# Fill pieces in cycles of four attention steps

## The chip, the cores and the metric

The kernel runs on one core of a Trainium2 chip. The metric is the time of one execution on the device, in microseconds (us). TensorE does the matmuls, ScalarE the exponentials, VectorE and GpSimd (POOL in the profile) the elementwise work; SyncE (SP) and GpSimd issue transfers.

## The reference

Two layers, each an attention block and a Fourier block, on x of 2048 rows and 640 columns, in fp32. There are 32 heads of 20 columns.

```python
def _A_ref(x, wqkv, wo):
    qkv = (x @ wqkv).reshape(B, S, 3, H, Dh).transpose(2, 0, 3, 1, 4)
    q, k, v = qkv[0], qkv[1], qkv[2]
    scores = jnp.einsum("bhqd,bhkd->bhqk", q, k) * (Dh ** -0.5)
    p = softmax(scores, axis=-1)
    o = jnp.einsum("bhqk,bhkd->bhqd", p, v)
    return o.transpose(0, 2, 1, 3).reshape(B, S, D) @ wo

def _B_ref(x, dft_seq_re, dft_seq_im, dft_hid_re, dft_hid_im):
    a = jnp.einsum("bsd,ed->bse", x, dft_hid_re)
    b = jnp.einsum("bsd,ed->bse", x, dft_hid_im)
    return jnp.einsum("ts,bse->bte", dft_seq_re, a) - jnp.einsum("ts,bse->bte", dft_seq_im, b)

for _ in range(2):
    x = x + _A_ref(layernorm(x), wqkv, wo)
    x = x + _B_ref(layernorm(x), dft_seq_re, dft_seq_im, dft_hid_re, dft_hid_im)
```

## The kernel before

A layer begins with a prologue (layer norm, transposes, the first two chunks of q and k, the first half of v), goes on with the attention sweep, and ends with the output projection and the Fourier block. The change touches the sweep alone.

**Steps.** The sweep has 512 steps. A step is a group `g` of four heads, a query block `qb` of 512 rows and a key chunk `kc` of 128 rows; `kc` runs fastest, then `qb`, then `g`. So a query block has 16 steps and a group has 64.

**Scores.** A step has two score tiles (`scores(n, j)`, two heads each). A tile is two matmuls at line 518, 62 rows deep and 512 columns wide, into one of three PSUM places `p0` to `p2`. ScalarE makes the exponential of the tile at line 521, into one of seven slots `e0` to `e6`. A score tile can start when the exponential of the third tile before it has left its place; an exponential can start when the values of the seventh tile before it have been taken.

**Values.** `values(n)` multiplies the exponentials of a step with v (line 529), for four heads side by side, and adds them up in `acc` over the 16 steps of a query block. In the program these are four matmuls for a step; the profile shows eight. At the last step `finish` transposes, divides and writes the block out.

**Fill work.** Only part of q, k and v exists when the sweep begins. The generator `work` makes the rest in pieces, on TensorE, between the steps: eight chunks of 128 columns of q or k, for four blocks of 512 rows each (15 matmuls of 512 columns for one block), and the second half of v, for 16 row tiles (15 matmuls of 320 columns for each). A piece is what `next(work)` issues; `s.blocks` counts them. All use one PSUM place, `fill`. After the last piece of a q or k block VectorE makes the two parts and the squares (`keep`), and some steps later `after` issues a norm matmul (line 212) and a reduction, from which the bound of the scores is made. At the end of a chunk it also splits the next weights and fetches those after them.

**Order.** All instructions stand in the order in which the program issues them; each engine waits with semaphores. `sweep` goes through the steps: two score tiles; then `fill(n)`, which may issue a piece; then values of earlier steps. Up to step `THIN = 236` the pieces go by `marks` (16 pieces up to step 44, 74 up to step 236), a block's pieces close together; while a block is unfinished (`more`) the values of a step are left for the next one, so that two steps of values come together. From step 236 on a piece comes at three places of each query block, and values follow by another rule.

**Loads.** `begin` and `sweep` also issue, at fixed `kc`, the loads of the next q and k tiles (`qload`, `kload`) on SyncE's queue, and `need` issues pieces at once where a group's chunk isn't made in time. `LATE` holds the groups whose last q chunk need only have its first 512 rows when the group starts. For these the bound is made again for each query block, and the q tiles of the next block are loaded at `kc` 10, not 4. Before, `LATE` is (4, 6).

`compare` issues VectorE's check of the Fourier matrices, spread over the steps. It was called with `fill` by `between`.

Of the kernel before, what the change touches and what calls it, by code (L numbers as in the profile page):

```python
# [23 lines left out]
GUARD = 30.0  # L24
NP = NT // 2
NQ = NT // 4
LATE = (256 // (4 * DH) + 1, 512 // (4 * DH))
FIRST = (0, 1, 4, 5)
HD = D // 2
TOL = 2.0 ** -32  # L30
# [5 lines left out]
def mha_fnet_kernel(ctx, tc, x_in, wqk, wv, wo, seq, hid, nat_seq, nat_hid, out):  # L36
# [65 lines left out]
    def pieces(blocks, n):  # L102

        todo = [f for b in blocks for f in b]
        for i in range(0, len(todo), n):
            for f in todo[i:i + n]:
                f()
            yield i + n < len(todo)
# [23 lines left out]
    class Qkv:  # L132
# [248 lines left out]
        def work(s):  # L381

            order = [ND + 1, 1, ND + 2, 2, ND + 3, 3, ND + 4, 4]
            w = {0: s.w1}

            def chunk(i):
                c = order[i]
                for tb in range(NB):
                    p = bank("fill", [128, 512], "pqk")
                    for more in pieces([s.product(p, w[i], tb, dc) for dc in range(ND)], 8 if (i, tb) < (5, 1) else 5):  # L390
                        if more:
                            yield True
                    sq = s.keep(p, c, tb, True, s.fill)

                    def after():
                        s.norms(bank("fill", [H, 512], "pn"), c, tb, sq)
                        s.made.add((c, tb))
                        if tb == NB - 1:
                            s.made.add(c)
                            if i + 1 < len(order):  # L400
                                w[i + 1] = s.weights(s.fill("w", [2, ND, 128], F32R, "wqk"), order[i + 1], True)
                            if i + 2 < len(order):
                                s.fetch(order[i + 2])
                    yield after

            for i in range(4):
                yield from chunk(i)
            for t in range(NT):
                p = bank("fill", [128, HD], "pv")
                for more in pieces([s.value(p, t, dc) for dc in range(ND)], 8):  # L410
                    if more:
                        yield True
                s.own(p, t, 1, True)
                yield None
            s.made.add("v")
            for i in range(4, 8):
                yield from chunk(i)

            s.silent = True
            r = s.bounds()  # L420
            ok = const.tile([128, 1], F32, name="ok", bufs=2)
            V.tensor_scalar(ok[:H], r[:H, 2:3], (GUARD / SCALE) ** 2, None, op0=OP.is_le)

            def after():
                p = bank("fill", [1, 1], "pok")
                PE.matmul(p, ok[:H], one[:H], start=True, stop=True)
                V.tensor_scalar(s.flag, p, float(H), None, op0=OP.is_equal)
            yield after
# [25 lines left out]
    class Attention:  # L454
# [95 lines left out]
                    G.dma_start(s.o[k, h * DH:(h + 1) * DH, qb * 512:(qb + 1) * 512],  # L550
                                hl[k][32 * j:32 * j + DH])

        def sweep(s, shift, begin, fill):
            done = calm = 0
            for n, (g, qb, kc) in enumerate(s.steps):
                begin(n, g, qb, kc)
                last = qb == NB - 1
                if kc == (7 if last else 10 if g in LATE else 4) and not (last and g == H // 4 - 1):
                    s.qload(*((g, qb + 1) if not last else (g + 1, 0)), shift)
                if last and g + 1 < H // 4:  # L560
                    for f, j in {1: [(0, 0)], 9: [(0, 1)], 11: [(1, 0)]}.get(kc, []):
                        s.kload(g + 1, f, j)
                if qb == 0 and kc == 0 and g:
                    s.kload(g, 1, 1)
                s.scores(n, 0)
                s.scores(n, 1)

                more, owed = fill(n) and n >= 2 and n + 1 < len(s.steps), n - 1 - done  # L570
                if n < s.THIN:
                    if more and kc != 1:
                        continue
                    count = owed
                else:
                    if more and owed < 3:
                        calm = n + 2
                        continue
                    count = min(owed, 1)
                    if owed > 1 and (done + 1) % NT and n >= calm:  # L580
                        calm = n + 2
                        count = 2
                for _ in range(count):
                    s.values(done)
                    done += 1
            for n in range(done, len(s.steps)):
                s.values(n)

        def run(s, done, project, check):

            work, tasks, later = s.a.work(), s.a.vweights(1, s.a.fill, pause=[lambda: None] * 2), list(check)
            s.work, s.blocks, s.after, s.rest, s.more, s.landed = True, 0, None, 0, False, 0

            marks = ((0, 0), (44, 16), (s.THIN, 74))

            def due(n):
                for (n0, k0), (n1, k1) in zip(marks, marks[1:]):
                    if n < n1:
                        return s.blocks < k0 + (k1 - k0) * (n - n0) / (n1 - n0)
                return s.blocks < 74 or s.blocks >= 107 or (n - 1) % NT in (2, 7, 12)  # L600

            def block(n):
                try:
                    f = next(work)
                    s.blocks += 1
                    s.more = f is True
                    s.after = (n + (2 if n < s.THIN else 4), f) if f and not s.more else None
                    s.rest = s.after[0] + 2 if s.after else n
                except StopIteration:
                    s.work = False  # L610
                    tasks.extend(done())

            def fill(n):
                if s.after:
                    if n >= s.after[0]:
                        f, s.after = s.after[1], None
                        f()
                elif s.work and n >= s.rest and (s.more and n < s.THIN or due(n + 1)):
                    block(n)
                    s.rest = max(s.rest, n + 2)  # L620
                    return s.work and not s.a.silent

            def compare(n):


                if n < 8:
                    return
                for _ in range(2):
                    if not later or n < s.landed or (len(check) - len(later)) * 490 >= n * len(check):
                        break  # L630
                    task = later.pop(0)
                    if isinstance(task, tuple):
                        s.landed = n + 5
                        task = task[1]
                    task()

            def need(n, *keys):
                while not all(k in s.a.made for k in keys):
                    if s.after:
                        fill(s.after[0])  # L640
                    else:
                        block(n)

            def begin(n, g, qb, kc):


                if qb == NB - 1 and g + 1 < H // 4:
                    when, to = 0, g + 1
                    c0, c1 = to * 80 // 128, ((to + 1) * 80 - 1) // 128
                    keys = [c0, (c1, 0) if to in LATE else c1, ND + c0, ND + c1] + (["v"] if to >= 4 else [])  # L650
                else:
                    when, to, keys = 5, g, [(((g + 1) * 80 - 1) // 128, qb + 1)]
                if to != g or g in LATE and qb < NB - 1:
                    if kc == when:
                        need(n, *keys)
                        s.shift = s.a.bound(to, s.room)
                    if kc - when in (0, 3, 5):
                        next(s.shift)

                if tasks and n % 2 == 0 and n >= 16 and n % 64 < 54:  # L660
                    tasks.pop(0)()
                for f in project.early.get(n, []):
                    f()

            def between(n):
                more = fill(n)
                compare(n)
                return more

            s.sweep("b", begin, between)  # L670
            assert not s.work and not later and not tasks, (len(later), len(tasks))

        def general(s, done, project):
# [35 lines left out]
                for j in range(2):  # L709
                    s.kload(0, f_, j)  # L710
            s.qload(0, 0, "m")
            s.sweep("m", lambda *_: None, lambda *_: None)
            for f in sum(project.early.values(), []):
                f()

# [813 lines left out]
```

## Time and profile before

| | |
|---|---|
| median of 3 runs | 2512.57 us (2512.54 to 2512.91) |
| the profiled execution | 2511.93 us, of which the span in the profile is 2510.1 |
| granted TensorE clock, mean | 0.999 |
| TensorE busy | 2479.9 us of the span |
| ScalarE busy | 2133.1 us |
| VectorE busy | 980.2 us |
| exponentials | 2048, 1934.4 us busy together |

Busy time of TensorE counts matmuls that are pipelined, so what a group of matmuls costs is better read from the distance between starts. In the profile's rows PE is TensorE, ACT ScalarE, DVE VectorE; a row of the timeline gives the start, the time to the end of the last, the engine, the line, what is written and read, the shape and the count; in brackets the idle time before it and what ended that. A row of the windows gives, for a stretch, the busy time of each engine (and the count of instructions), the granted TensorE clock, the share of the transfer engines and GB/s.

### The profile page before, as it was taken

The numbers are of one execution on the slowest core, as the hardware profiler recorded it, in microseconds if no ns is written. First come the engines' busy times: TensorE is split into PE (matmuls) and PEld (weight loads), VectorE is DVE, ScalarE is ACT, GpSimd is POOL, SyncE is SP. The second block draws the span as 40 slices with busy tenths as digits, with TensorE's granted clock in tenths as the row PEclk, the third lists the DMA queues.
The fourth block names the chain that finished last, engine by engine and source line by source line (L and its number), as shares of the span: only waits on it lengthen the run. The fifth ranks groups of instructions, "written<-read, shape, count | busy, mean of one in ns | idle before, by whom it ended". The sixth has DMA issues, their size and how long they took to land. (4 is left out here: it accounts for less than half of the span.)

```text
span 2510.1 us, 43669 instructions
## 1 busy us (share of the span) xinstructions
PE 2479.9 (99%) x16350; PEld 1147.5 (46%) x16350; DVE 980.2 (39%) x2144; ACT 2133.1 (85%) x2430; POOL 524.1 (21%) x1028
## 2 busy tenths in 40 slices
PE   8999999999999999999999999999999999999998
PEld 7644434433333332249885444444433333322596
DVE  6245422234243333416753444223233333332275
ACT  6688899989999999985457888999899999999752
POOL 2012111111212212113321121111121122221233
PEclk9999999999999999999999999999999999999999
DMA  5224221223222224327553332212131322233355
GB/s 188 95 88 126 81 90 44 83 72 94 86 90 86 94 86 123 118 89 245 190 182 100 114 111 91 80 57 65 59 100 51 92 62 71 58 108 96 115 211 195
DMA packets 127241, 262.58 MB, mean 105 GB/s; under 512 B 28952, under 2 KB 53304, under 8 KB 127020
## 3 DMA queue, kind: packets, MB, share of 16 engines
q1 hardware_dynamic: 88428, 159.83, 19.7%
q0 software_dynamic: 38592, 99.85, 12.6%
q8 instruction: 132, 2.16, 0.4%
q14 instruction: 89, 0.73, 0.1%
HBM read 175.29 MB, written 84.26 MB: 103 GB/s over the span
## 5 line engine op out<-in xcount | busy, mean ns | idle before, releaser
L521 ACT ACTIVATE e<-psc 128x1024 f32<-128x1024 f32 x2048 | 1934.4, 1121 | 126.0 <-PE psc L518 94.1
L529 PE MATMUL acc<-e,v 128*32 128x512 f32 x8192 | 1057.9, 602 | 3.9 <-DVE of L536 3.8
L518 PE MATMUL psc<-stq,stk 62*128 62x512 f32 x4096 | 786.2, 455 | 1.3 <-ACT e L521 1.3
L518 PEld LDWEIGHTS psc<-stq,stk 62*128 62x128 f32 x4096 | 335.5, 184 | 792.3 <-ACT e L521 762.6
L529 PEld LDWEIGHTS acc<-e,v 128*32 128x32 f32 x8192 | 188.9, 108 | 381.6 <-issue 358.4
L99 PE MATMUL pqk<-xt,wqk 128*128 128x512 f32 x1200 | 319.6, 407 | 2.1 <-DVE top L213 1.4
L550 POOL DMA_DIRECT2D o<-oh x256 | 131.5, 522 | 872.5 <-DVE oh L545 871.4
L84 DVE CAST hl<-pqk 128x512 fp32r<-128x512 f32 x64 | 44.3, 692 | 553.5 <-PE pqk L99 553.5
L99 PEld LDWEIGHTS pqk<-xt,wqk 128*128 128x128 f32 x1200 | 213.2, 188 | 90.3 <-issue 43.5
L536 DVE STREAM_TRANSPOSE of<-acc 128x512 f32<-128x512 f32 x64 | 45.8, 716 | 349.9 <-PE acc L529 349.3
L99 PE MATMUL pv<-wv,xt 128*128 128x320 f32 x960 | 159.7, 316 | 0.0
L99 PEld LDWEIGHTS pv<-wv,xt 128*128 128x128 f32 x960 | 141.1, 188 | 24.7 <-issue 21.2
L550 POOL DMA_DIRECT2D o<-ot x256 | 128.5, 510 | 1.9 <-issue 1.4
L207 POOL DMA_DIRECT2D scrq<-hl x40 | 28.1, 704 | 446.1 <-DVE hl L87 311.4
L243 DVE COPY v<-pv 128x320 f32<-128x320 f32 x32 | 15.7, 491 | 235.3 <-PE pv L99 235.3
L765 DVE TENSOR_REDUCE far<-cq 128x1 f32<-128x512 f32 (+5 forms) x169 | 98.5, 584 | 5.7
L92 PE MATMUL py<-wo,o 128*128 128x320 f32 x320 | 99.1, 310 | 1.4 <-DVE xr L947 1.4
L207 POOL DMA_DIRECT2D scrk<-hl x40 | 28.0, 699 | 344.3 <-DVE hl L87 300.2
L93 PE MATMUL py<-wo,o 128*128 128x320 f32 x320 | 98.6, 308 | 0.0
L94 PE MATMUL py<-wo,o 128*128 128x320 f32 x320 | 98.6, 308 | 0.0
L769 DVE TENSOR_TENSOR cq<-cq 128x512 f32<-128x512 f32 (+4 forms) x166 | 96.4, 580 | 2.4 <-DMA cq<-in_nat_seq_dram 2.4
L213 DVE TENSOR_REDUCE top<-pn 32x1 f32<-32x512 f32 x80 | 53.5, 676 | 107.4 <-PE pn L212 107.4
(200 smaller groups left out, 1729.2 us busy)
## 6 DMA issues: line engine op xcount, KB each, us to landing
cq<-in_nat_seq_dram POOLq DMA_DIRECT2D x64, 512.0 KB, 5.3
scrq<-hl POOLq DMA_DIRECT2D x40, 512.0 KB, 3.2
scrk<-hl POOLq DMA_DIRECT2D x40, 512.0 KB, 3.2
stq<-scrq SPq DMA_DIRECT2D x256, 80.0 KB
stk<-scrk SPq DMA_DIRECT2D x128, 160.0 KB
o<-o SPq DMA_DIRECT2D x16, 1280.0 KB
stq<-scrq SPq DMA_DIRECT2D x256, 40.0 KB
stk<-scrk SPq DMA_DIRECT2D x128, 80.0 KB
```

The costliest lines, as they stand in the source:

```text
L92: PE.matmul(out_ap, ah, bh, start=start, stop=False)
L93: PE.matmul(out_ap, ah, bl, start=False, stop=False)
L94: PE.matmul(out_ap, al, bh, start=False, stop=stop)
L99: yield lambda i=i, j=j, k=k: PE.matmul(out_ap, a[i], b[j], start=dc == 0 and k == 0, stop=dc == ND - 1 and k == 2)
L207: G.dma_start(s.scr["qk"[k]][c * 128:(c + 1) * 128, :, tb * 512:(tb + 1) * 512], hl.bitcast(F32))
L213: V.tensor_reduce(s.top[:H, c // ND, c % ND, tb:tb + 1], p, op=OP.max, axis=AX.X)
L518: PE.matmul(p[:, i], s.k[g, kc // 8, j][r, kc % 8 * 128:(kc % 8 + 1) * 128], s.q[g, qb, j][r], start=True, stop=True)
L521: A.activation(e, p, AF.Exp, scale=SCALE)
L529: PE.matmul(s.acc[32 * j:32 * j + 32], s.a.v[kc][:, v0:v0 + 32], s.e[n, j // 2][:, j % 2], start=kc == 0, stop=kc == NT - 1, skip_group_ch ...
L550: G.dma_start(s.o[k, h * DH:(h + 1) * DH, qb * 512:(qb + 1) * 512], hl[k][32 * j:32 * j + DH])
L765: V.tensor_reduce(to, x, op=OP.max, axis=AX.X, apply_absolute_value=True)
L769: V.tensor_tensor(y, x, y, op=op)
```

## The change

`sweep` takes a `plan`. Where `plan(n)` gives a piece, four steps go as one cycle: three score tiles, the piece, three score tiles, values of two steps, two score tiles, the waiting `after` if there is one, values of two steps. `plan` gives one at steps 1, 5, 9 and so on, up to step 229, for the first 58 pieces. A v block is one piece of 15 matmuls, not one of 8 and one of 7, so there are 58 pieces up to that point where there were 74. Pieces outside the cycles come from step 236 on, as before. `LATE` has group 1 too, since the chunk of its last head is made later than before.

```diff
-LATE = (256 // (4 * DH) + 1, 512 // (4 * DH))
+LATE = (1, 4, 6)
...
-                for more in pieces([s.value(p, t, dc) for dc in range(ND)], 8):
+                for more in pieces([s.value(p, t, dc) for dc in range(ND)], 15):
...
+            while n < len(s.steps):
+                opened(n)
+                piece = plan and plan(n)
+                if piece:
+
+                    for t in range(8):
+                        m, j = n + t // 2, t % 2
+                        if t and not j:
+                            opened(m)
+                        s.scores(m, j)
+                        if t == 2:
+                            piece()
+                        if t == 7:
+                            fill(m)
+                        if j:
+                            compare(m)
+                        if t in (5, 7):
+                            for _ in range(2):
+                                s.values(done)
+                                done += 1
+                    n += 4
+                    continue
                 s.scores(n, 0)
                 s.scores(n, 1)
                 more, owed = fill(n) and n >= 2 and n + 1 < len(s.steps), n - 1 - done
-                if n < s.THIN:
-                    if more and kc != 1:
-                        continue
-                    count = owed
+                compare(n)
+                n += 1
+                if plan and n <= s.THIN:
+                    count = owed + 1
+                elif more and owed < 3:
+                    calm = n + 1
+                    continue
...
-            marks = ((0, 0), (44, 16), (s.THIN, 74))
...
-                return s.blocks < 74 or s.blocks >= 107 or (n - 1) % NT in (2, 7, 12)
+                return s.blocks < 58 or s.blocks >= 91 or (n - 1) % NT in (2, 7, 12)
...
-                elif s.work and n >= s.rest and (s.more and n < s.THIN or due(n + 1)):
+                elif s.work and n >= max(s.rest, s.THIN) and due(n + 1):
...
+            def plan(n):
+                if n % 4 == 1 and n + 3 < s.THIN and s.blocks < 58 and not s.after:
+                    return lambda: block(n + 1)
...
-            s.sweep("b", begin, between)
+            s.sweep("b", begin, fill, plan, compare)
```

`opened(n)` holds what stood at the head of the loop: `begin` and the loads of a step.

More of the change, by code (lines that the diff above doesn't have):

```diff
@@ L551, in finish, with sweep, opened @@
                                 hl[k][32 * j:32 * j + DH])
-        def sweep(s, shift, begin, fill):
-            done = calm = 0
-            for n, (g, qb, kc) in enumerate(s.steps):
+        def sweep(s, shift, begin, fill=lambda n: None, plan=None, compare=lambda n: None):
+            done = calm = n = 0
+            def opened(n):
+                g, qb, kc = s.steps[n]
                 begin(n, g, qb, kc)
@@ L570, in sweep @@
                 more, owed = fill(n) and n >= 2 and n + 1 < len(s.steps), n - 1 - done
-                if n < s.THIN:
-                    if more and kc != 1:
-                        continue
-                    count = owed
-                else:
-                    if more and owed < 3:
-                        calm = n + 2
-                        continue
+                compare(n)
[5 more added lines that the diff above has]
+                    continue
+                else:
                     count = min(owed, 1)
-                    if owed > 1 and (done + 1) % NT and n >= calm:
-                        calm = n + 2
+                    if owed > 1 and (done + 1) % NT and n > calm:
+                        calm = n + 1
                         count = 2
@@ L592, in run @@
             s.work, s.blocks, s.after, s.rest, s.more, s.landed = True, 0, None, 0, False, 0
-            marks = ((0, 0), (44, 16), (s.THIN, 74))
             def due(n):
-                for (n0, k0), (n1, k1) in zip(marks, marks[1:]):
-                    if n < n1:
-                        return s.blocks < k0 + (k1 - k0) * (n - n0) / (n1 - n0)
-                return s.blocks < 74 or s.blocks >= 107 or (n - 1) % NT in (2, 7, 12)
+                return s.blocks < 58 or s.blocks >= 91 or (n - 1) % NT in (2, 7, 12)
             def block(n):
@@ L663, in begin @@
                     f()
[L665 to L668, printed above, removed]
-            s.sweep("b", begin, between)
+            s.sweep("b", begin, fill, plan, compare)
             assert not s.work and not later and not tasks, (len(later), len(tasks))
@@ L711, in general @@
             s.qload(0, 0, "m")
-            s.sweep("m", lambda *_: None, lambda *_: None)
+            s.sweep("m", lambda *_: None)
             for f in sum(project.early.values(), []):
```

## The prediction

> **What bounds the kernel now.** I read the page first, for the engine that is never idle.
>
> ```profile
> span 2510.1 us, 43669 instructions
> ...
> PE 2479.9 (99%) x16350; PEld 1147.5 (46%) x16350; DVE 980.2 (39%) x2144; ACT 2133.1 (85%) x2430; POOL 524.1 (21%) x1028
> ```
>
> TensorE at 99% may still be an average over stages with different limits, so the second view was the windows. I cut them at the first score matmul of step 0, at that of step 233 (the first step after the new cycles) and at the end of the sweep; the last row is the early window of the second layer.
>
> ```profile
> core 0: us, PE busy (x) PEld busy (x) DVE busy (x) ACT busy (x) POOL busy (x), PEclk, DMA share, GB/s
> 86.62:593.31 506.69, 503.61 (x3357) 208.83 (x3357) 184.86 (x375) 448.60 (x467) 87.69 (x156) 1.00 0.27 85
> 593.31:1117.20 523.89, 523.67 (x3543) 173.68 (x3539) 182.59 (x399) 518.87 (x559) 101.21 (x182) 1.00 0.30 93
> 1330.24:1837.20 506.96, 503.32 (x3357) 208.68 (x3357) 180.66 (x350) 448.87 (x467) 88.81 (x158) 1.00 0.28 86
> ```
>
> In the early window ScalarE works 448.60 of 506.69 us, TensorE nearly always. In the later one ScalarE works 518.87 of 523.89 us: there the exponentials are the limit. The changed cycles lie wholly in the early window, where TensorE's order decides; what follows keeps its limit. So a microsecond of TensorE time saved before step 233 moves all that follows by a microsecond, as long as ScalarE does not become the limit of the early window too.
>
> The third view is the timeline of TensorE alone, over two q/k pieces. Its columns are the start, the time to the end, and the count; what a group costs is the distance to the next start, since matmuls overlap.
>
> ```profile
> 99.89 2.11 PE L99 MATMUL pqk<-xt,wqk 128*128 128x512 f32 x8
> 101.92 0.73 PE L518 MATMUL psc<-stq,stk 62*128 62x512 f32 x4
> 102.59 1.92 PE L529 MATMUL acc<-e,v 128*32 128x512 f32 x16
> 104.44 0.73 PE L518 MATMUL psc<-stq,stk 62*128 62x512 f32 x4
> 105.10 1.88 PE L99 MATMUL pqk<-xt,wqk 128*128 128x512 f32 x7
> 106.91 0.73 PE L518 MATMUL psc<-stq,stk 62*128 62x512 f32 x4
> 107.57 1.92 PE L529 MATMUL acc<-e,v 128*32 128x512 f32 x16
> 109.43 0.73 PE L518 MATMUL psc<-stq,stk 62*128 62x512 f32 x4
> 110.09 0.39 PE L212 MATMUL pn<-sq,ind 128*32 128x512 bf16 x1
> 110.10 1.24 PE L529 MATMUL acc<-e,v 128*32 128x512 f32 x8
> 111.27 0.73 PE L518 MATMUL psc<-stq,stk 62*128 62x512 f32 x4
> 111.93 1.06 PE L529 MATMUL acc<-e,v 128*32 128x512 f32 x8
> 112.92 0.73 PE L518 MATMUL psc<-stq,stk 62*128 62x512 f32 x4
> ```
>
> From start to start: two score tiles 0.66 us (104.44 to 105.10); values of one step 0.99 (111.93 to 112.92), of two steps 1.85 (102.59 to 104.44); a q or k piece of eight 2.03 (99.89 to 101.92), of seven 1.81 (105.10 to 106.91); the norm matmul lengthens the values behind it from 0.99 to 1.17 (110.10 to 111.27), so 0.18. Two values together cost 0.13 less than twice one: a change from one kind of work to another costs something that a longer run does not pay again. That is what the change collects. The groups lie end to end; TensorE hardly waits here.
>
> **The new cycle, term by term.** A cycle is 3 score tiles, piece, 3 score tiles, 2 values, 2 score tiles, 2 values: four steps and one piece. By the order of TensorE's instructions there are 58 of them, steps 1 to 232: 21 with eight q/k matmuls, 21 with seven and a norm, 16 with a whole v block of fifteen. The same work was in 74 pieces before; the steps, tiles and matmuls are as many.
>
> A run of three score tiles stands in the trace near a layer's start, with a wait behind it that is needed below.
>
> ```profile
> 86.62 0.73 PE L518 MATMUL psc<-stq,stk 62*128 62x512 f32 x4
> ...
> 89.35 0.98 PE L518 MATMUL psc<-stq,stk 62*128 62x512 f32 x6
> 90.97 0.50 PE L518 MATMUL psc<-stq,stk 62*128 62x512 f32 x2 [0.65 <-ACT e L521]
> 91.40 1.88 PE L99 MATMUL pqk<-xt,wqk 128*128 128x512 f32 x7
> ...
> 93.87 1.92 PE L529 MATMUL acc<-e,v 128*32 128x512 f32 x16
> 95.73 0.73 PE L518 MATMUL psc<-stq,stk 62*128 62x512 f32 x4
> ```
>
> ScalarE in the same stretch:
>
> ```profile
> 87.19 1.94 ACT L521 ACTIVATE e<-psc 128x1024 f32<-128x1024 f32 x2
> 89.90 4.88 ACT L521 ACTIVATE e<-psc 128x1024 f32<-128x1024 f32 x5 [0.77 <-PE psc L518]
> 95.03 1.02 ACT L521 ACTIVATE e<-psc 128x1024 f32<-128x1024 f32 x1 [0.26 <-PE acc L529]
> 96.33 5.61 ACT L521 ACTIVATE e<-psc 128x1024 f32<-128x1024 f32 x6 [0.27 <-PE psc L518]
> ```
>
> Six score matmuls last 0.98, four 0.73: the third tile adds 0.25, so three tiles cost 0.66 + 0.25 = 0.91. The other bound for it is 0.33, half of a pair.
>
> A v block of fifteen is not in this sweep, but its halves are:
>
> ```profile
> 311.71 1.29 PE L99 MATMUL pv<-wv,xt 128*128 128x320 f32 x7
> 312.93 0.73 PE L518 MATMUL psc<-stq,stk 62*128 62x512 f32 x4
> ...
> 321.23 1.43 PE L99 MATMUL pv<-wv,xt 128*128 128x320 f32 x8
> 322.60 0.73 PE L518 MATMUL psc<-stq,stk 62*128 62x512 f32 x4
> ```
>
> Seven cost 1.22, eight 1.37; the eighth adds 0.15 by the starts and 0.14 by the lengths. Fifteen cost 1.22 + 8 x 0.145 = 2.38, against 2.59 for the halves.
>
> TensorE alone then needs 0.91 + P + 0.91 + 1.85 + 0.66 + 1.85 = 6.18 + P: 8.21 with eight, 7.99 with seven, 8.56 with a v block.
>
> ScalarE has to fit in. There are three score banks, so a cycle's sixth tile waits until the third tile's exponential has ended. The first exponential starts 0.60 after its score (95.73 to 96.33). Six in a row take 5.61, one alone 1.02, so each further one (5.61 - 1.02) / 5 = 0.918; the third ends at 0.60 + 2 x 0.918 + 1.02 = 3.46 after the cycle's start. At 90.97 a tile waited in this way for the exponential that began at 89.90 and ended at 90.92: it started 0.05 later. So the sixth tile may start at 3.51. TensorE would reach it at 0.91 + P + 0.58, where 0.58 is 0.91 less one tile: 3.52 with eight, no wait; 3.30 with seven, a wait of 0.21; 3.87 with a v block, none. From a tile that waited to what follows it is 0.43 (90.97 to 91.40), not 0.33. So the seven-cycle costs 3.51 + 0.43 + 4.36 = 8.30 (4.36 are the two pairs of values and the two tiles between them), not 7.99. This wait is new; behind it on TensorE stand those values and tiles, and nobody else waits for them but ScalarE.
>
> The sixth tile's exponential also needs one of the seven slots for exponentials, which the first values free 1.16 after they begin (93.87 to 95.03): at 3.94 + 1.16 = 5.10. ScalarE reaches it at 0.60 + 5 x 0.918 = 5.19 anyway. The eighth starts at 3.94 + 1.85 + 0.60 + 0.918 = 7.31, and ScalarE is free at 8.23, while the next cycle's first exponential is not ready before 8.30 + 0.60. These 0.7 us of slack in each cycle are why ScalarE does not set its length.
>
> The sum for a layer: 21 x (8.21 + 8.30 + 0.18) = 350.5 and 16 x 8.56 = 137.0, together 487.5. Step 0 runs ahead of the first cycle: five score tiles in a row, of which the fifth waits for the second exponential. That ends at 87.19 + 1.94 = 89.13, and 0.05 + 0.43 later the piece starts, at 89.61; in a settled cycle it starts 0.91 after the cycle, so step 0 costs 89.61 - 0.91 - 86.62 = 2.08. Step 233 then comes 489.6 us after step 0, where it took 506.69 and 506.96. **Gain: 17.1 and 17.4 us in the two layers, 34.5 in all.**
>
> **What else moves.** Behind step 233 there is no piece until step 237, as before, and the same work is left. The new order has one step of values fewer owed there, 0.85 us for each layer (1.85 - 0.99) if TensorE is still late at that point: not counted, kept for the lower end.
>
> The norm matmul waits for squares that VectorE makes of the piece. It comes 0.91 + 1.85 + 0.66 = 3.42 behind the seven, before 0.66 + 1.85 + 0.66 = 3.17. VectorE is busy 185 of 507 us in this window; if in that share of cases the norm came late by as much as it lasts, 0.39, it would be 21 x 0.36 x 0.39 = 2.9 us for each layer, an upper end. I take nothing, since the norms get more time than they had.
>
> A query block ends on the last values of a cycle, with six score tiles and the piece between them and the accumulator's next use, so its evacuation is hidden; with values of two blocks back to back it would stand between them. v is complete at step 192 and needed at step 240.
>
> Group 1's q tiles are late now: its bound is made again for each query block, three times more in a layer, and the loads are issued at step 10 of 16 and not 4, behind the bound's own transfer on SyncE's queue. Group 4 does that already:
>
> ```profile
> 655.30 0.24 SPq L499 DMA_DIRECT2D stq<-shiftb  x1
> ...
> 666.72 0.73 PE L518 MATMUL psc<-stq,stk 62*128 62x512 f32 x4
> ```
>
> The last of the twelve loads is issued at 655.30, the scores that need them start at 666.72: 11.4 us to spare, landing included. Group 1's blocks are no shorter (four cycles, 33 us). So I take nothing for it.
>
> The profiled execution took 2511.93 us for its span of 2510.1; the median of the runs is 2512.57. 2511.93 - 34.5 = 2477.4; on the median, 2512.57 - 34.5 = 2478.1. I forecast **2478 us**. Under 0.2% (5 us) could not be told from no change here.
>
> **Rivals.**
>
> *The ring of three banks does not bind* (12%): with the first exponential at 0.55 (89.35 to 89.90) instead of 0.60, or a restart that overlaps the wait, the seven-cycles come near 7.99. Worth up to 21 x 0.31 = 6.5 for each layer: 2465, and 2463 with the value step already done.
>
> *Longer runs save less* (17%): the third tile at 0.33 makes both runs of three 0.08 longer, 0.16 a cycle where no wait hides it, (21 + 16) x 0.16 = 5.9 for each layer: 2490. If the eight-cycles too pay the restart of 0.1, 2494; with late norms besides, 2500. For it: the three-tile run stands only once in a layer. Against it: its length of 0.98.
>
> *It is refilled* (3%): a further wait of 0.30 in each of the 58 cycles takes the whole gain, 2512. Exponentials that do not overlap, 1.02 each, would give all q/k cycles 0.60 + 2 x 1.02 + 1.02 + 0.05 + 0.43 + 4.36 = 8.50 and still leave 7 us of gain in each layer; nothing in the rows shows more.
>
> *Late q tiles* (5%), slower: three block starts of group 1 in each layer. Its loads share SyncE's queue with the weights' fetches, which wait for VectorE. They have 11 us to spare; beyond that each microsecond costs six, so 17 us later the gain is gone, and 22 us later the time is 2478 + 6 x 10.6 = 2542. Group 4's rows speak against it.
>
> *The clock falls* (3%), slower: were the wait in the seven-cycles to lower TensorE's clock to half, each microsecond at that clock would lose half of one. At 34 us of a layer's 490 the gain is gone; at a fifth of them, 98 us, the time is 2478 + 98 = 2576. Against it: the granted clock is 1.00 in all windows, the later one too, where TensorE's scores wait for ScalarE. The Trainium skill, "TensorE: Matmul & The Clock Gate", section "A second HAM failure mode: psum-queue depth-cycling", tells of small idle gaps between matmul groups, from cycling through the PSUM banks, that made the clock swing to half. By that rule the new order, with its wait on a bank, would be the slower one; the later window's 1.00 does not agree with it.
>
> **How the numbers follow.** Forecast 60%, its rivals 12, 17, 3, 5 and 3. Faster: 60 + 12 + 17 = 89%; same 3%; slower 8%. The range goes from 2463 (no bank wait, one value step less) to 2497 (the third tile at its bound, restarts, part of the late norms). It leaves out the last three rivals and the far ends of the first two, under two in ten.
>
> **What would show it.** Between the first scores of steps 0 and 233, 490 us instead of 507, in both layers; groups of six score matmuls 0.91 from start to start, a v block 2.38; a wait for the exponential ahead of the sixth tile in the seven-cycles, 0.2 us, and none in the v cycles; the stretch from step 233 on within 1 us of 523.9. A sixth tile that waits in all cycles, group 1's scores waiting for a transfer at a block's start, or a granted clock under 1.00 would make it wrong.

## The result, and the profile after

The changed kernel takes 2483.94 us (median of 4 runs, 2483.46 to 2485.32), the kernel before 2512.56 beside it: a ratio of 0.9887, 95% interval 0.987 to 0.9904. It is faster by 28.6 us, where 34.5 were forecast. The profiled execution has a span of 2481.4 us.

The windows of the changed kernel, cut at the same points as before: the first score matmul of step 0, that of step 233, and the end of the sweep, in both layers.

```profile
core 0: us, PE busy (x) PEld busy (x) DVE busy (x) ACT busy (x) POOL busy (x), PEclk, DMA share, GB/s
86.55:579.88 493.33, 490.26 (x3365) 220.08 (x3364) 188.09 (x391) 441.74 (x467) 90.91 (x161) 1.00 0.29 89
579.88:1103.53 523.65, 523.43 (x3531) 173.60 (x3530) 181.54 (x397) 518.48 (x558) 99.37 (x179) 1.00 0.30 92
1316.29:1808.16 491.87, 489.46 (x3365) 220.11 (x3365) 183.87 (x368) 442.20 (x467) 90.83 (x161) 1.00 0.29 90
1808.16:2331.90 523.74, 523.51 (x3533) 173.61 (x3532) 158.05 (x390) 518.48 (x558) 102.71 (x191) 1.00 0.25 74
```

The early windows are 13.4 and 15.1 us shorter (506.69 and 506.96 before), 28.4 together; the span is shorter by 28.7. The later windows have hardly moved (523.89 before, 523.65 and 523.74 now), and the clock stays at 1.00. So all but 0.3 us of the gain lies between step 0 and step 233, as forecast, and the question is only how long a cycle is there.

Two cycles on TensorE, one with eight matmuls and one with seven and a norm:

```profile
105.38 0.96 PE L518 MATMUL psc<-stq,stk 62*128 62x512 f32 x6
106.28 2.11 PE L99 MATMUL pqk<-xt,wqk 128*128 128x512 f32 x8
108.32 1.07 PE L518 MATMUL psc<-stq,stk 62*128 62x512 f32 x6
109.32 1.92 PE L529 MATMUL acc<-e,v 128*32 128x512 f32 x16
111.17 0.73 PE L518 MATMUL psc<-stq,stk 62*128 62x512 f32 x4
111.84 1.92 PE L529 MATMUL acc<-e,v 128*32 128x512 f32 x16
113.69 0.96 PE L518 MATMUL psc<-stq,stk 62*128 62x512 f32 x6
114.58 1.89 PE L99 MATMUL pqk<-xt,wqk 128*128 128x512 f32 x7
116.40 1.30 PE L518 MATMUL psc<-stq,stk 62*128 62x512 f32 x6
117.63 1.92 PE L529 MATMUL acc<-e,v 128*32 128x512 f32 x16
119.49 0.73 PE L518 MATMUL psc<-stq,stk 62*128 62x512 f32 x4
120.15 0.39 PE L212 MATMUL pn<-sq,ind 128*32 128x512 bf16 x1
120.16 2.10 PE L529 MATMUL acc<-e,v 128*32 128x512 f32 x16
122.19 0.97 PE L518 MATMUL psc<-stq,stk 62*128 62x512 f32 x6
```

A run of three tiles ahead of a piece lasts 0.96 to 0.97 and costs 0.89 to 0.90. The run behind the seven lasts 1.30: the wait that was forecast stands inside it (start to start 1.23, so 0.33 more than 0.90). The run behind the eight lasts 1.07 and costs 1.00, 0.10 more, where none was forecast. The eight-cycle is 113.69 - 105.38 = 8.31 us, the seven-cycle with its norm 122.19 - 113.69 = 8.50.

A v cycle has no such wait (its first three groups cost 0.89, 2.40 and 0.89), 367.12 - 358.57 = 8.55:

```profile
358.57 0.96 PE L518 MATMUL psc<-stq,stk 62*128 62x512 f32 x6
359.46 2.46 PE L99 MATMUL pv<-wv,xt 128*128 128x320 f32 x15
361.86 0.96 PE L518 MATMUL psc<-stq,stk 62*128 62x512 f32 x6
...
367.12 0.96 PE L518 MATMUL psc<-stq,stk 62*128 62x512 f32 x6
```

ScalarE over the same two q/k cycles: it goes through the piece with hardly a gap (eight exponentials in one row) and idles 0.6 to 0.7 us at a cycle's start.

```profile
105.98 7.73 ACT L521 ACTIVATE e<-psc 128x1024 f32<-128x1024 f32 x8 [0.74 <-PE psc L518]
114.29 5.61 ACT L521 ACTIVATE e<-psc 128x1024 f32<-128x1024 f32 x6 [0.58 <-PE psc L518]
120.12 1.94 ACT L521 ACTIVATE e<-psc 128x1024 f32<-128x1024 f32 x2 [0.22 <-PE psc L518]
122.78 2.86 ACT L521 ACTIVATE e<-psc 128x1024 f32<-128x1024 f32 x3 [0.73 <-PE psc L518]
```

### The profile page after: what moved, and what is told of

Same layout as the page of the kernel before. It is cut to its first block, busy times and chain, and to the rows that moved or that the text cites. A ratio compares the mean times of both kernels' runs of the same rounds, so it can differ in the third digit from the quotient of the medians.

```text
span 2481.4 us, 43743 instructions
## 1 busy us (share of the span) xinstructions
PE 2451.9 (99%) x16350; PEld 1170.1 (47%) x16350; DVE 984.7 (40%) x2174; ACT 2118.3 (85%) x2430; POOL 527.4 (21%) x1034
## 5 line engine op out<-in xcount | busy, mean ns | idle before, releaser
L529 PE MATMUL acc<-e,v 128*32 128x512 f32 x8192 | 1041.6, 601 | 0.4 <-DVE of L536 0.4
L518 PE MATMUL psc<-stq,stk 62*128 62x512 f32 x4096 | 770.4, 452 | 5.5 <-ACT e L521 1.9
L529 PEld LDWEIGHTS acc<-e,v 128*32 128x32 f32 x8192 | 207.7, 108 | 380.3 <-issue 348.6
L99 PE MATMUL pv<-wv,xt 128*128 128x320 f32 x960 | 151.3, 313 | 0.0
```

Of the source, the lines that this page charges most:

```text
L99: yield lambda i=i, j=j, k=k: PE.matmul(out_ap, a[i], b[j], start=dc == 0 and k == 0, stop=dc == ND - 1 and k == 2)
L518: PE.matmul(p[:, i], s.k[g, kc // 8, j][r, kc % 8 * 128:(kc % 8 + 1) * 128], s.q[g, qb, j][r], start=True, stop=True)
L529: PE.matmul(s.acc[32 * j:32 * j + 32], s.a.v[kc][:, v0:v0 + 32], s.e[n, j // 2][:, j % 2], start=kc == 0, stop=kc == NT - 1, skip_group_ch ...
```

## The experiments

In what follows a run is an unbroken row of matmuls of one kind on TensorE (scores, values, a piece, a norm). The theory: starting a run costs 0.1 to 0.2 us, the change starts fewer of them, and what it does not gain is taken by the sixth score tile's wait for the third exponential. Each kernel was timed beside the kernel before on the same chip, but not all on one chip: the kernel before took 2511.8 us beside four of them and 2512.6 to 2512.7 beside the others, so two rows compare to about 1 us. The stage is the time from the first score matmul of step 0 to that of step 233 in the profiles; the last column counts its runs in the order of TensorE's instructions.

| kernel | median us | ratio to before, interval | stage, layer 1 and 2 | runs in a stage |
|---|---|---|---|---|
| before | 2512.56 | | 506.7, 507.0 | 486 |
| changed | 2483.94 | 0.9887 (0.987 to 0.9904) | 493.3, 491.9 | 369 |
| v blocks whole, alone | 2519.57 | 1.0031 (1.0019 to 1.0042) | 508.9, 509.0 | 485 |
| group 1 late, alone | 2511.97 | 1.000 (0.999 to 1.0009) | 506.6, 506.9 | 486 |
| two tiles ahead of the piece | 2525.82 | 1.0055 (1.0038 to 1.0071) | 513.3, 513.8 | 485 |
| pieces of ten and five | 2496.46 | 0.994 (0.9923 to 0.9956) | 499.0, 499.0 | 369 |
| extra behind the 2nd exponential | 2492.53 | 0.9924 (0.9907 to 0.994) | 496.0, 496.2 | 369 |
| extra behind the 8th exponential | 2484.62 | 0.9887 (0.9871 to 0.9904) | 493.6, 492.1 | 369 |
| three tiles ahead, runs as many as with two | 2502.7 | 0.9961 (0.9946 to 0.9975) | 502.1, 502.1 | 485 |

**Pieces of ten and five** (against the changed kernel)

```diff
-... 8 if (i, tb) < (5, 1) else 5):
+... 10 if (i, tb) < (5, 1) else 5):
```

> The changed kernel with the fifteen matmuls of a q or k block cut into ten and five, not eight and seven; nothing else. The theory (a cycle is not shorter than 8.31, since its sixth score tile waits for the third one's exponential, which ends at 3.46): with ten the piece takes 2.51 and the cycle 0.89 + 2.51 + 0.89 + 4.36 = 8.65, with five TensorE needs 7.5 and waits up to 8.31. So 0.34 x 21 = 7.1 us more for each layer, 2498 in all, and a wait of 0.7 us ahead of the sixth tile in the five-cycles. A rival (TensorE's own work sets the length of all cycles, and what is missing of the forecast gain was lost elsewhere): the same matmuls in the same cycles, 2484.

```profile
105.91 0.96 PE L518 MATMUL psc<-stq,stk 62*128 62x512 f32 x6
106.81 2.56 PE L99 MATMUL pqk<-xt,wqk 128*128 128x512 f32 x10
...
114.56 0.96 PE L518 MATMUL psc<-stq,stk 62*128 62x512 f32 x6
115.45 1.42 PE L99 MATMUL pqk<-xt,wqk 128*128 128x512 f32 x5
116.81 0.85 PE L518 MATMUL psc<-stq,stk 62*128 62x512 f32 x4
118.07 0.50 PE L518 MATMUL psc<-stq,stk 62*128 62x512 f32 x2 [0.41 <-ACT e L521]
118.50 1.92 PE L529 MATMUL acc<-e,v 128*32 128x512 f32 x16
```

The ten-cycle takes 114.56 - 105.91 = 8.65 us. In the five-cycle the sixth tile stands apart, with ScalarE named for its wait; it starts 118.07 - 114.56 = 3.51 after the cycle's start, as it does behind seven and behind eight. The wait is 0.7 us, as expected: after the fifth tile the sixth could follow at 117.39, and comes at 118.07. The same matmuls in the same cycles cost 12.5 us more in all (14 expected). In the second layer's stage it is 7.2 us, where 7.1 was worked out; in the first it is 5.7, because five exponentials that start late in the changed kernel (below) start late here too, but ahead of ten matmuls, where they cost nothing. So a q/k cycle has a floor, and work under it is free.

**A small exponential more, in two places** (against the changed kernel)

```diff
                         s.scores(m, j)
+                        if t == 1:
+                            A.activation(extra, ident[:, :16], AF.Exp, scale=SCALE)
...
+    extra = const.tile([128, 16], F32, name="extra")
```

In the other kernel it is `t == 7`.

> The changed kernel with a small exponential more on ScalarE in each of the 58 cycles, behind the second tile's: 128 x 16 elements of a constant, which nobody reads. It takes x, 0.1 to 0.2 us. The theory (the third exponential's end holds the sixth score tile): each q/k cycle is longer by x, 8.31 + x, the v cycles, whose sixth tile comes 0.35 after that end, keep 8.56. 42 x x for each layer, with x = 0.15 that is 6.3, 12.6 in all: 2497 (2492 to 2501). A rival (TensorE is the limit and ScalarE has 0.7 us to spare in each cycle): 2484.

> The changed kernel with the same small exponential more in each cycle, but behind the eighth tile's, where ScalarE waits 0.5 us for the next cycle's first score. The theory: no change, 2484 within 1 us; where on ScalarE the time is added decides, not how much. A rival (ScalarE as a whole is close to the limit of the cycles): as behind the second, 2492 or more.

Behind the second, ScalarE and then TensorE:

```profile
107.00 1.94 ACT L521 ACTIVATE e<-psc 128x1024 f32<-128x1024 f32 x2 [0.74 <-PE psc L518]
108.83 0.22 ACT L579 ACTIVATE extra<-ident 128x16 f32<-128x16 f32 x1
108.93 5.89 ACT L521 ACTIVATE e<-psc 128x1024 f32<-128x1024 f32 x6
```

```profile
106.40 0.96 PE L518 MATMUL psc<-stq,stk 62*128 62x512 f32 x6
107.29 2.11 PE L99 MATMUL pqk<-xt,wqk 128*128 128x512 f32 x8
109.33 1.18 PE L518 MATMUL psc<-stq,stk 62*128 62x512 f32 x6
...
114.81 0.96 PE L518 MATMUL psc<-stq,stk 62*128 62x512 f32 x6
```

Behind the eighth, ScalarE:

```profile
107.23 0.22 ACT L579 ACTIVATE extra<-ident 128x16 f32<-128x16 f32 x1
108.07 7.73 ACT L521 ACTIVATE e<-psc 128x1024 f32<-128x1024 f32 x8 [0.62 <-PE psc L518]
```

The operation lasts 0.22 and moves the third exponential by 0.10 (it starts 108.93 - 106.40 = 2.53 into the cycle, 2.43 in the changed kernel). The eight-cycle grows by the same 0.10, to 114.81 - 106.40 = 8.41, and the seven-cycle by 0.09. Over 42 q/k cycles and two layers that is about 8 us; the medians differ by 2492.53 - 2483.94 = 8.6. That the two agree so well is partly luck: the stages differ by 2.7 and 4.3 us. The first layer's would by 4.1, but the five late exponentials of the changed kernel (below), worth 1.4 us, do not occur in this one. The other 1.6 us lie outside the stages, 1.0 of them ahead of the first score (87.51 and 86.55), which the theory has nothing to say of. The same operation behind the eighth falls into ScalarE's gap and costs nothing that can be told from zero (0.7 us in the medians, 0.3 and 0.2 in the stages). That the third exponential sets the length of the q/k cycles is shown, and that ScalarE's total does not.

**Two tiles ahead of the piece** (against the changed kernel)

```diff
-                        if t == 2:
+                        if t == 1:
                             piece()
...
-                        if t in (5, 7):
-                            for _ in range(2):
+                        for _ in range({3: 2, 5: 1, 7: 1}.get(t, 0)):
...
```

> The changed kernel with another order within its cycle: 2 score tiles, piece, 2 score tiles, 2 values, 2 score tiles, 1 values, 2 score tiles, 1 values. The pieces stay where they are (one in four steps, v blocks whole); the runs are as short as before. The theory (runs): 4 x 0.66 + P + 1.85 + 2 x 0.99 = 6.47 + P: 8.51 with eight matmuls, 8.28 + 0.18 with seven and the norm, 8.86 with a v block; 21 x 16.97 + 16 x 8.86 = 498.1 and step 0: about 500 us from step 0 to step 233, 7 to 8 more than in the changed kernel (493.3 and 491.9), 2499 in all. The wait on the score banks should be gone from the piece's cycle. A rival (the gain comes from the even spacing of the pieces, not from the runs): 2484, as the changed kernel.

It missed by 27 us, and stands slower than before. The wait on the banks is gone, as expected, but another has come. TensorE at the end of an eight-cycle (fifth and sixth tile, values, last two tiles, values, next cycle), and ScalarE in it:

```profile
110.72 0.73 PE L518 MATMUL psc<-stq,stk 62*128 62x512 f32 x4
...
112.37 0.73 PE L518 MATMUL psc<-stq,stk 62*128 62x512 f32 x4
113.03 1.32 PE L529 MATMUL acc<-e,v 128*32 128x512 f32 x8
114.29 0.73 PE L518 MATMUL psc<-stq,stk 62*128 62x512 f32 x4
```

```profile
108.80 1.94 ACT L521 ACTIVATE e<-psc 128x1024 f32<-128x1024 f32 x2 [0.68 <-PE psc L518]
111.31 5.61 ACT L521 ACTIVATE e<-psc 128x1024 f32<-128x1024 f32 x6 [0.58 <-PE psc L518]
```

The last values of the cycle cost 1.26 instead of 0.99. Added up over all starts of a layer, TensorE's runs account for 501 us of this stage, as worked out; 12 more are waits, nearly all inside values. These values read the fifth and the sixth tile. The fifth tile's exponential starts as soon as its score allows (110.72 to 111.31, with ScalarE idle before it), and the sixth's ends two exponentials later, at 113.25. TensorE comes to the values at 113.03, 2.31 after the fifth tile; for the two heads of the sixth tile it loads the weights only at 113.31:

```profile
113.31 0.14 PEld L529 LDWEIGHTS acc<-e,v 128*32 128x32 f32 x4
```

So the values stand too close behind their score tiles. ScalarE also runs dry during the piece (0.68 before the row at 108.80), but this wait does not depend on it: ScalarE idles there 0.45 us with seven matmuls, 0.68 with eight and 1.03 with a v block (medians), and in all three kinds of cycle the next run starts 1.03 to 1.04 after the sixth exponential's end.

**Three tiles ahead, runs as many as with two** (against the changed kernel)

```diff
-                        if t in (5, 7):
-                            for _ in range(2):
-                                s.values(done)
-                                done += 1
+                        for _ in range({4: 1, 5: 1, 7: 2}.get(t, 0)):
+                            s.values(done)
+                            done += 1
```

> The changed kernel with a third order within its cycle: 3 score tiles, piece, 2 score tiles, 1 values, 1 score tile, 1 values, 2 score tiles, 2 values. It has as many runs on TensorE as the order with two tiles ahead of the piece (four of scores, three of values, one piece), but three tiles ahead of it, so ScalarE has work while the piece runs. That other order took 513 us from step 0 to step 233, where its runs alone account for 501; its values waited for exponentials. If the reason is that ScalarE runs dry during a piece with two tiles ahead, this order is nearly free of those waits: 8.52 a q/k cycle, 8.89 a v cycle, 503 us for each layer with the norms, 2504 in all. If the number of runs decides what lies between 2526 and 2484, or something else in the wait of the values: 2526, as the other order.

```profile
106.50 5.78 ACT L521 ACTIVATE e<-psc 128x1024 f32<-128x1024 f32 x6 [0.73 <-PE psc L518]
```

ScalarE now works through the piece (six in a row), and the kernel takes 2502.7 us, against 2504 expected and 2526 for the other order with as many runs. The number came out, but the reason given for it was not the one at work. This order differs from the other in a second thing: the values that read the fifth and sixth tile come 4.29 us behind the fifth, not 2.32, and the sixth exponential ends 3.12 behind it. By the rows of the other order that is what takes the wait away. The experiment by itself does not separate the two, since it changes both.

Of the 42 us between that order and the changed kernel, 23 are thus waits inside values (the stages differ by 11.2 and 11.7). The other 19 are a difference of two things. With 485 runs in a stage and not 369, TensorE's runs take about 19 us longer in each layer; 9 to 11 of these come back, because this order hardly waits on the banks. Against the kernel before, which has as many runs, it gains 10 us: that one waits about 6 us in a stage, this one about 1.

**v blocks whole, alone** (against the kernel before)

```diff
-                for more in pieces([s.value(p, t, dc) for dc in range(ND)], 8):
+                for more in pieces([s.value(p, t, dc) for dc in range(ND)], 15):
...
-            marks = ((0, 0), (44, 16), (s.THIN, 74))
+            marks = ((0, 0), (44, 16), (s.THIN, 58))
...
-                return s.blocks < 74 or s.blocks >= 107 or (n - 1) % NT in (2, 7, 12)
+                return s.blocks < 58 or s.blocks >= 91 or (n - 1) % NT in (2, 7, 12)
```

> The kernel before with one part of the change alone: a v block is one piece of fifteen matmuls, and the marks count 58 pieces where they counted 74. The theory (the gain is what starting a run of one kind of work costs on TensorE, paid less often): a block costs 2.39 us and not 1.37 + 1.22, so 0.20 less, 16 times; but with a piece fewer a block, values of two steps come together 57 times and not 71, which costs 14 x 0.14 again. 16 x 0.20 - 14 x 0.14 = 1.2 us a layer, 2.5 in all: 2510. A rival (merging the v pieces is a large share of the gain of 28.6): a third of it, 2503 or less.

Both missed: it is slower by 7.8 us. The stages are 2.2 and 2.0 us longer. By the sum of starts, TensorE's runs are about 1.0 us shorter in a layer, as expected, while its scores wait 7.9 and 7.1 us, not 4.7 and 4.3.

These waits are not at the long pieces. The edit does more than merge: with 58 pieces counted up to step 236 and not 74, the q/k blocks behind step 54 come every eight to ten steps, where they came every six or seven. Of the first layer's waits 1.6 us lie between the first and last v piece, where it was 2.9, and 6.3 in the stretches of q and k, where it was 1.8. There TensorE's scores wait while ScalarE works without a gap:

```profile
283.36 0.87 PE L518 MATMUL psc<-stq,stk 62*128 62x512 f32 x4
284.16 1.06 PE L529 MATMUL acc<-e,v 128*32 128x512 f32 x8
```

```profile
278.99 9.28 ACT L521 ACTIVATE e<-psc 128x1024 f32<-128x1024 f32 x10 [0.50 <-PE psc L518]
```

The two tiles cost 0.80 and not 0.66. A step without a piece needs 0.66 + 0.99 = 1.65 on TensorE and 2 x 0.918 = 1.84 on ScalarE, so it is ScalarE's pace that such steps come to when many follow one another; this last is worked out, and no experiment shows it alone. What the merged piece is worth at the old spacing no experiment shows either. Of the rest of the 7.8 us, 0.6 lie between the layers and about 2.4 behind the last matmul; what makes these is open.

**Group 1 late, alone** (against the kernel before)

```diff
-LATE = (256 // (4 * DH) + 1, 512 // (4 * DH))
+LATE = (1, 4, 6)
```

> The kernel before with another part alone: group 1 among those whose q tiles are loaded late, so that its bound is made three times more in a layer. The theory: the loads land 10 us before they are needed and the small work lies on engines with time to spare, so no change: 2512.6, within 1 us. A rival (the bound's extra work or the later loads cost part of the gain, and explain that it was 28.6 us and not 34.5): 2515 or more.

2511.97 beside 2511.8: no change. The late loads and the bounds made again cost nothing here.

## Why the prediction was right

**What bounds what.** Right: the stage from step 0 to step 233 shrank, the rest did not, and the time followed one to one (28.4 of 28.6 us).

**The terms.** The run of three was worth 0.90 where 0.91 was worked out, the v block 2.40 where it was 2.38, the v cycle 8.55 to 8.56 where it was 8.56. The start of the sweep cost 86.55 to 89.53 up to the first piece, 2.98, where 2.99 was worked out.

**The wait on the banks.** Right in place and size: the sixth tile starts 3.51 after the cycle's start, the number worked out, and the seven-cycle with its norm takes 8.50, worked out as 8.48. The two places of the extra exponential and the pieces of ten and five show the cause.

**The term that was mis-sized.** "3.52 with eight, no wait": TensorE reaches the sixth tile at the very moment at which it may start, and there the restart of 0.43 in place of 0.33 is paid all the same. The eight-cycle takes 8.31, not 8.21. It is so in 20 of the 21 eight-cycles of each layer (the first, behind step 0, reaches its sixth tile later), which makes 4.0 of the 6.0 us that the two stages are longer than forecast, and it is what the second rival had named in passing ("if the eight-cycles too pay the restart of 0.1"). The rows of the weight loader (PEld) show why. In an eight-cycle the load of the sixth tile's weights itself waits for the exponential, and goes in together with the matmul; in a v cycle it comes 0.23 ahead:

```profile
108.89 0.18 PEld L518 LDWEIGHTS psc<-stq,stk 62*128 62x128 f32 x2 [0.28 <-ACT e L521]
108.89 0.50 PE L518 MATMUL psc<-stq,stk 62*128 62x512 f32 x2
...
362.20 0.19 PEld L518 LDWEIGHTS psc<-stq,stk 62*128 62x128 f32 x2
362.43 0.39 PE L518 MATMUL psc<-stq,stk 62*128 62x512 f32 x2
```

From the sixth tile to what follows it is 0.43 in the first and 0.32 in the second. Two v cycles of the first layer, at steps 153 and 185, lie between: their exponential ends late, the load comes 0.07 ahead, and it is 0.36. So "no wait" was worked out for the matmul, and its load had to be free before it. With ten matmuls, where the tile is reached late enough, the restart is gone: 8.65 is 0.90 + 2.49 + 0.89 + 4.37.

Another 0.02 in each seven-cycle makes 0.6 us in all. The last 1.4 us are five eight-cycles of the first layer, at steps 25, 57, 89, 121 and 217, of 8.58 to 8.61. In these the first exponential starts about 0.88 after its score and not 0.60 (so it does at steps 153 and 185, the v cycles named above):

```profile
139.87 2.86 ACT L521 ACTIVATE e<-psc 128x1024 f32<-128x1024 f32 x3 [1.03 <-PE psc L518]
```

ScalarE idles 1.03 there, not 0.73; the 0.28 goes through to the cycle, as the theory has it. The late starts lie 32 steps apart; why they come is open, and the second layer has none of them.

**What was reasoned too narrowly.** The gain was put down to starting runs less often. By the sum of starts that holds between these two kernels: the runs of the changed kernel, 369 and not 486, are about 19 us shorter in a layer, and its waits are about 6 and 4 us longer. Why TensorE takes longer when a run starts, no experiment shows. The forecast also looked at ScalarE ("ScalarE has to fit in") for the banks, the slots and its total, but did not ask whether the values find their exponentials done. In this order they do, by 0.8 us or more in every cycle; in the order with two tiles ahead they do not, and that alone costs 12 us in each layer.

**The rivals.** That the ring does not bind fell with the seven-cycles; late q tiles fell with the kernel that has that part alone; the clock was 1.00 in all four windows, with a wait on a bank in nearly every q/k cycle. The swing to half that the Trainium skill describes ("TensorE: Matmul & The Clock Gate", section "A second HAM failure mode: psum-queue depth-cycling") did not come.

## What to carry to other kernels

When TensorE and ScalarE share a loop, follow one cycle on both engines, with the start of each tile and each exponential; a wait that is shorter than the engine's slack in total can still set the cycle's length, and only its place tells. When an order of work is made, count the time on the first engine between a tile and the work that reads its result, and beside it the time that the second engine needs for it. Where a sum says that a wait is exactly zero, ask whether the load that goes ahead of the matmul is free of it too. And where a part of a change is tried alone, see what else its edit moves: here the spacing of the other pieces.

## What the runs showed of the hardware

An operation of 0.22 us on ScalarE between two exponentials moved the next by 0.10: in a row it cost less than it lasted. A score tile cost 0.32 to what followed it when its weights were loaded 0.23 ahead of its matmul, 0.36 with the load 0.07 ahead, and 0.43 when the load had waited and went in with it. With the same matmuls, 116 fewer runs made TensorE's runs in a stage about 19 us shorter, about 0.16 us for each.
